# Bulk loads at the change of pass behind small transfers, and one segment's first maxima behind the next group's first products

## The chip, the cores and the metric

One Trainium2 chip, of which one core is used. The metric is the device time of one execution in microseconds, taken in several runs; the time before is the median of three runs. A profile comes from one execution of its own.

TensorE (PE, with its weight loads as PEld), VectorE (DVE), ScalarE (ACT) and GpSimd (POOL) each work through a list of instructions in order. All transfers of this kernel are issued by SyncE (SP), also in order, and run on 16 DMA engines. Semaphores tie the lists together.

## The reference

An attention block with a memory of the earlier segments, and a token-mixing MLP, both behind a layer norm that is scaled and shifted by values computed from a condition `c`:

```python
h = _layernorm(x, axis=-1) * (1 + ca) + sa
x = x + ga * _A_ref(h, A_wq, A_wk, A_wv, A_wo, A_beta)
h = _layernorm(x, axis=-1) * (1 + cb) + sb
x = x + gb * _B_ref(h, B_w1, B_b1, B_w2, B_b2)
```

There are 2048 tokens of 1024 channels. In `_A_ref`, 32 heads of width 32 work on 4 segments of 512 tokens. For each head and segment: causal softmax attention inside the segment; a read of the memory, `phi(q) @ M / phi(q) @ z`; a mix of both by a gate for each head; then the memory takes up this segment's keys and values. `_B_ref` multiplies across tokens, 2048 to 3584 and back, with a gelu between. Everything is float32.

## The kernel before, in words

Float32 precision is got from TensorE's faster formats by splitting: an operand becomes a high and a low part (`split`, lines 115 to 122: ScalarE or VectorE rounds the high part, VectorE or GpSimd subtracts for the low part), and a product is three products: high by high, high by low, low by high.

**Iterations.** The attention stage runs over `its` (line 376): two passes, in each 8 groups of 4 heads, in each group two segments. The first pass (t = 0 to 15) takes the first and second segment, the second pass (t = 16 to 31) the third and fourth. So t = 3 is group 1, segment 1, and t = 4 is group 2, segment 0. Between t = 15 and t = 16 is the change of pass: the normalized input of the third segment must be in the on-chip pages instead of the first's, and the weights of group 0 are loaded again.

**One iteration** consists of:
- `project(t, 0)` and `project(t, 1)`: keys and values of two token tiles each, tile `nps`, made of 8 chunks (`kv_chunk`, line 188) of six products. Chunk k uses page `h` of channel block k and weight tile k // 2. Line 195 is the product.
- `project(t, 2)`: transposes of the keys (`kps`, line 419), the queries (`qps`, line 203), their splits into the tile `sg`, which has one buffer, and for each head the *stack*: `stack(t, h)` (lines 382 to 390) issues three transfers `sk<-sg` of 128 KB (L388, L389, L390) that put the parts of q and k of one head on one set of partitions. `project(t, 3)` has the stack of the last head and prepares the values. There are two sets of `sk` tiles, used by even and odd t in turn.
- `maxima(t, h)` (line 482): for each head the scores are computed once (`sx`, `sy`, `sz`, line 492), only to find each query's maximum with VectorE (line 494). For every two heads the maxima are transposed (`nmps`), split (`nt`), and sent by four small transfers `sk<-nt` of 2 KB (line 507) into two spare rows of `sk`.
- `scores(t, h)` (line 521): the scores again, transposed, with the maxima subtracted through the spare rows (`a`, lines 529, 532, 536), the exponential on ScalarE, a mask by GpSimd, a copy `ph` (line 543, ScalarE) and the low part `p` (line 545, GpSimd).
- `values(t, h)` (line 547): products `pv` of `ph` and `p` with the values (line 563), normalized by VectorE.

**Bulk transfers at the change of pass.** `reload_h(seg, ct)` (line 371) loads one page of 512 KB, queue entry `h<-hT` (L373); eight are a segment. A page of the third segment takes the buffer of a page of the first, so it cannot be loaded before t = 14's products have read that. `load_w` (line 178) loads a group's six weight tiles, `wv<-wsp` and `wq<-wsp` (L170), 512 KB each; weight tiles have eight buffers. `mod_fetch(j)` (line 586) loads 512 KB of the modulation weights, `rawm` (L588), into one of three buffers given out in turn; `mod_late` (line 591) reduces it with VectorE.

**What sets the order.** One Python loop over n (lines 707 to 735) traces the program: for each n `scores(n)`, `maxima(n + 3)`, `values(n - 2)`, perhaps `load_w`, `project(n + 8)`, perhaps `reload_h`, and planned work such as `mod_fetch(2)` at n = 51 and `mod_fetch(3)` at n = 52. The order in which an engine or the queue gets its instructions is not this one: a planner in the compiler lays it, by when it expects inputs and buffers to be ready, earlier traced work first. `with tc.issue_after(x)` keeps what is traced inside the block behind instruction x on x's own engine or queue; it adds no instruction. `last_sk[t, h]` is the last transfer of a stack, `last_nt[t, h]` the last of the four small transfers.

Of the kernel before, what the change touches and what calls it, by code (L numbers as in the profile page):

```python
# [18 lines left out]
P = 128  # L19
NSEG, L = 4, 512  # L20
NK = D // P
# [20 lines left out]
def attention_and_mlp(ctx, tc, x, wq, wkv, wo, beta, w1, b1, w2, b2, c, wm_a, wm_b, out):  # L42
    nc = tc.nc
    V, A, G, T, SY = nc.vector, nc.scalar, nc.gpsimd, nc.tensor, nc.sync
# [143 lines left out]
    def kv_chunk(w, h, half, k, ps):  # L188
        wt = w["v", k // 2]
        o = 256 * (k % 2)  # L190
        n = 6 * k
        for i, j in ((0, 0), (0, 1), (1, 0)):
            for aa in range(2):
                tt = 2 * half + aa
                T.matmul(ps[:, aa], h[:, j, 128 * tt:128 * tt + 128], wt[:, i, o:o + 256],  # L195
                         start=(n == 0), stop=(n >= 6 * NK - 2), skip_group_check=True)
                n += 1

    def q_chunk(w, h, k, ps):
        wt = w["q", k // 4]  # L200
        o = 128 * (k % 4)
        for n, (i, j) in enumerate(((0, 0), (0, 1), (1, 0))):
            T.matmul(ps, wt[:, i, o:o + 128], h[:, j], start=(k + n == 0), stop=(3 * k + n == 3 * NK - 1))  # L203
# [130 lines left out]
    for i in range(2):  # L334
        ps = bank("s2", 2, f"scps{i}")
# [35 lines left out]
    def reload_h(seg, ct):  # L371
        pg = new_page(f"h{seg}_{ct}")
        SY.dma_start(pg.bitcast(F32), hT1[seg - 2, ct])  # L373
        hpages[seg, ct] = pg
# [2 lines left out]
    NI = len(its)  # L377
    st = {}

    last_sk, last_nt = {}, {}  # L380

    def stack(t, h):

# [8 lines left out]
    def project(t, piece):  # L392
        pr, g, seg = its[t]
        if piece == 0:
            st[t] = {}
        w = W[pr, g]
        hp = [hpages[seg, ct] for ct in range(NK)]
        d = st[t]
        if piece in (0, 1):
            if piece == 0:  # L400
                d["k32"] = pj.tile([P, 4, 128], F32, tag="k32", bufs=1, name=f"k32_{t}")
                d["v32"] = pj.tile([P, 4, 132], F32, tag="v32", bufs=1, name=f"v32_{t}")
                G.memset(d["v32"][:, :, 128:132], 1.0)
            half = piece
            k32, v32 = d["k32"], d["v32"]
            if t:
                ps = two_tiles(bank("pj", 2, f"nps{t}_{half}"))
                for k in range(NK):
                    kv_chunk(w, hp[k], half, k, ps)
            else:  # L410
                ps = two_tiles(first[half])
            A.copy(k32[:, 2 * half:2 * half + 2], ps[:, :, 0:128])
            A.copy(v32[:, 2 * half:2 * half + 2, 0:128], ps[:, :, 128:256])
        elif piece == 2:
            k32 = d["k32"]
            d["sg"] = sg = pj.tile([P, 4, L], F32R, tag="sg", bufs=1, name=f"sg{t}")
            ps = bank("pj", 2, f"kps{t}")
            for i in range(4):
                T.transpose(ps[:, 128 * i:128 * i + 128], k32[:, i], ident)
            split(sg[:, 2:4], ps, A, V)  # L420
            if t:
                ps = bank("pj", 2, f"qps{t}")
                for k in range(NK):
                    q_chunk(w, hp[k], k, ps)
            else:
                ps = first[2]
            split(sg[:, 0:2], ps, A, V)
            if seg:
                r = pj.tile([P, L], F32, tag="tmp", bufs=2, name=f"rq{t}")
                A.activation(r, ps, AF.Relu, scale=-1.0)  # L430
                A.activation(r, r, AF.Exp, scale=-1.0)
                d["pq"] = pj.tile([P, L], F32, tag="pq", bufs=1, name=f"pq{t}")
                V.scalar_tensor_tensor(d["pq"], ps, 0.0, r, op0=ALU.max, op1=ALU.add)
            if seg < 3:
                r = pj.tile([P, L], F32, tag="tmp", bufs=2, name=f"rk{t}")
                kf = k32.rearrange("p a n -> p (a n)")
                A.activation(r, kf, AF.Relu, scale=-1.0)
                A.activation(r, r, AF.Exp, scale=-1.0)
                d["pk"] = pj.tile([P, 4, 128], F32, tag="pk", bufs=1, name=f"pk{t}")
                V.scalar_tensor_tensor(d["pk"].rearrange("p a n -> p (a n)"), kf, 0.0, r, op0=ALU.max, op1=ALU.add)  # L440
            for h in range(3):
                stack(t, h)
        else:
            stack(t, 3)
            v = d["v32"][:, :, 0:128].rearrange("p a (h e) -> p a h e", h=4)
            vp = d["vp"] = b.tile([P, 4, 4, NV], BF16, tag="vp", bufs=3, name=f"vp{t}")
            r1 = pj.tile([P, 4, 4, 32], F32, tag="tmp", bufs=2, name=f"r1_{t}")
            G.memset(vp[:, :, :, 0:1], 1.0)
            A.copy(vp[:, :, :, 1:33], v)
            V.tensor_tensor(r1, v, vp[:, :, :, 1:33], op=ALU.subtract)  # L450
            A.copy(vp[:, :, :, 33:65], r1)
            V.tensor_tensor(vp[:, :, :, 65:97], r1, vp[:, :, :, 33:65], op=ALU.subtract)
            memory(t)
# [28 lines left out]
    def maxima(t, h):  # L482
        d = st[t]
        if h % 2 == 0:
            d["mx"] = b.tile([P, 2, 4], F32, tag="mx", bufs=2, name=f"mx{t}_{h}")
        mx = d["mx"]
        q, k = d["sk", h][0:96, 0], d["sk", h][0:96, 1]
        for tiles in ((0, 1), (2,), (3,)):
            s = bank("s1", 2, f"s{'xxyz'[tiles[-1]]}_{t}_{h}")
            outs = [(i, s[:, 128 * i * (len(tiles) - 1):][:, 0:128 * i + 128]) for i in tiles]  # L490
            for i, o in outs:
                T.matmul(o, q[:, 128 * i:128 * i + 128], k[:, 0:128 * i + 128], start=True, stop=True)  # L492
            for i, o in outs:
                marks[4 * t + h - LEADS, "V"] = V.tensor_tensor_reduce(  # L494
                    o, o, mask[:, 384 - 128 * i:], 1.0, -3.0e38, op0=ALU.add, op1=ALU.max,
                    accum_out=mx[:, h % 2, i:i + 1])
        if h % 2 == 0:
            return
        ps = bank("ms", 1, f"nmps{t}_{h}")
        T.transpose(ps[0:8, 0:128], mx.rearrange("p a b -> p (a b)"), ident)  # L500
        nt = [b.tile([8, P], F32R, tag=f"nt{i}", bufs=2, name=f"nt{i}_{t}_{h}") for i in range(2)]
        A.activation(nt[0], ps[0:8, 0:128], AF.Copy, scale=-1.0)
        V.scalar_tensor_tensor(nt[1], ps[0:8, 0:128], -1.0, nt[0].bitcast(F32), op0=ALU.mult, op1=ALU.subtract)
        for hh in range(2):
            sk = d["sk", h - 1 + hh]
            for part in range(2):
                last_nt[t, h] = SY.dma_start(sk[96 + part:97 + part, 0].bitcast(F32).rearrange("p (b n) -> p b n", n=128),
                             nt[part][4 * hh:4 * hh + 4].bitcast(F32))
# [76 lines left out]

    def mod_fetch(j):
        r = a.tile([P, D], F32, tag="raw", bufs=3, name=f"rawm{j}")
        SY.dma_start(r, wm_b[P * j:P * j + P])  # L588
        return r

    def mod_late(j, r):
# [98 lines left out]
    for g in range(2, NG):  # L690
        n = 8 * g - 13
# [7 lines left out]
    for j in range(32):  # L699
        n = 49 + j if j < 8 else ML0 + 2 * j + 8  # L700
        later(n, lambda j=j: mod_fetch(j), n + 1, lambda r, j=j: mod_late(j, r), "V")
    plan(WO0 - 3, lambda: spread(gaw, 0))
    for i in range(8):
        n = WO0 + WOS * i
        later(n, lambda i=i: wo_fetch(i), n + 1, lambda r, i=i: wo_split(i, r), "G")

    for n in range(-LEADS, 4 * NI + VL):
        at(scores, n)
        at(maxima, n + LEADS)
        with behind(n, "P" if n - VL >= 64 else ""):  # L710
            at(values, n - VL)
        m = n + LEADP
        if 0 <= m + 4 < 4 * NI:
            t = (m + 4) // 4
            if its[t][:2] not in W:
                with tc.issue_after(last_sk[t - 2 if t > 16 else 0, 3].ins):
                    load_w(its[t][1], its[t][0])
        if m >= 8:
            at(project, m)
        if 59 <= m < 67:  # L720
            seg, ct = 2 + (m - 59) // 4, 2 * ((m - 59) % 4)
            with ExitStack() as s:
                if seg == 3:
                    s.enter_context(tc.issue_after((last_sk[15, 3] if ct < 4 else last_nt[14, 3]).ins))
                reload_h(seg, ct)
                reload_h(seg, ct + 1)
        if 4 * NI - 5 <= m < 4 * NI + 3:
            i = m - 4 * NI + 5
            for c in (2 * (i % 4), 2 * (i % 4) + 1):
                wop[c, i // 4] = new_page(f"wo{c}_{i // 4}")  # L730
                if c < 5 or i < 4:
                    SY.dma_start(wop[c, i // 4].bitcast(F32), wos[c, i // 4])
        for f, engines in todo.pop(n, ()):
            with behind(n, engines):
                f()
# [14 lines left out]
    w = cw_pool.__enter__()  # L750
# [412 lines left out]
```

## Time and profile before

| | |
|---|---|
| time before, median of 3 runs | 2220.87 us (2216.29 to 2220.99) |
| profiled execution | 2220.33 us, span 2218.6 us |
| mean granted clock of TensorE | 0.998 |
| busy: TensorE, VectorE, ScalarE, GpSimd | 98%, 75%, 51%, 32% of the span |
| DMA | 423.05 MB, mean 191 GB/s |
| attention stage | from about 60 us to about 947 us, pass 2 from about 495 us |

A row of the timeline gives start, duration (for several instructions merged in one row, of all), engine, line, operation, tile written and tiles read, count, and in brackets how long the engine had stood idle before it and what ended that. "SPq" rows are transfers at the time at which the queue issues them; the issue takes the time shown, the landing is later. "Granted clock" is 1.00 at full speed. A stretch's busy time of TensorE can hide slow work: at half clock it is busy and does half.

### The profile page before, as it was taken

What the parts mean: (1) busy time and instruction counts of PE and PEld (TensorE: products, weight loads), DVE (VectorE), ACT (ScalarE), POOL (GpSimd) and SP (SyncE); (2) the same over time, 40 slices, a digit from 0 to 9 for tenths busy, and PEclk for the clock granted to TensorE, in tenths of its full rate; (3) what the DMA queues carried; (4) which work ended last, traced back from release to release, by engine and by line L of the source; (5) the groups of instructions that cost most, each with busy time, mean ns of one, the idle gap of its engine ahead of it and who ended that gap; (6) DMA issues with size and microseconds to landing.
All of it is one profiled execution on the core that took longest, in us unless ns stands there. A gap on an engine that the chain in (4) does not pass through costs nothing.

```text
span 2218.6 us, 38129 instructions
## 1 busy us (share of the span) xinstructions
PE 2183.0 (98%) x13786; PEld 1879.1 (85%) x13786; DVE 1674.1 (75%) x3762; ACT 1132.9 (51%) x2050; POOL 720.0 (32%) x831
## 2 busy tenths in 40 slices
PE   8999999999999999999999999999999999999999
PEld 5988998889999999988888888888888888888887
DVE  7687777767777686755858766888888887969687
ACT  5486876855666666654636533533334242424232
POOL 2175766656667677653002200033330000000000
PEclk9999999999999999999999999999999999999999
DMA  7656665587566666664755686665556541414134
GB/s 287 193 178 195 182 181 167 166 295 249 165 202 194 201 199 183 198 222 133 243 194 195 225 319 250 246 232 206 214 202 223 195 156 58 143 58 147 57 124 152
DMA packets 175184, 423.05 MB, mean 191 GB/s; under 512 B 17524, under 2 KB 71828, under 8 KB 166036
## 3 DMA queue, kind: packets, MB, share of 16 engines
q1 hardware_dynamic: 174996, 420.61, 57.4%
q8 instruction: 110, 1.80, 0.3%
q14 instruction: 78, 0.64, 0.1%
HBM read 244.62 MB, written 125.06 MB: 167 GB/s over the span
## 4 chain that ended last, share of the span: by engine, by line
PE 83%; DVE 7%; DMA 4%; ACT 2%; issue 1%; POOL 1%; SPq 1%; DVEq 0%; ACTq 0%
PE mx L943 48%; PE nps L195 10%; PE po L813 7%; PE qps L203 6%; PE pv L563 3%; DMA rawm<-in_wm_b_dram 2%; PE a L529 1%; PE sz L492 1%; PE sx L492 1%; POOL p L545 1%; DMA sk<-sg 1%; PE a L536 1%; DVE wv L122 1%; PE srow L308 1%; PE a L532 1%
## 5 line engine op out<-in xcount | busy, mean ns | idle before, releaser
L943 PE MATMUL mx<-bU,sp 128*128 128x512 f32 x2352 | 534.4, 389 | 0.9 <-DVE ac L950 0.9
L943 PEld LDWEIGHTS mx<-bU,sp 128*128 128x128 f32 x2352 | 441.1, 188 | 93.7 <-issue 1.3
L119 ACT CAST sp<-wr 128x384 fp32r<-128x384 f32 (+2 forms) x408 | 217.0, 545 | 429.9 <-PE mx L943 354.8
L195 PE MATMUL nps<-wv,h 128*128 128x256 f32 x3072 | 430.5, 283 | 1.5 <-DVE h L122 0.8
L943 PE MATMUL mx<-bA,sp 128*128 128x512 f32 x1764 | 430.5, 389 | 0.0
L545 POOL TENSOR_TENSOR p<-p,ph 128x640 f16<-128x640 f32 x256 | 376.7, 1472 | 119.8 <-ACT ph L543 115.0
L195 PEld LDWEIGHTS nps<-wv,h 128*128 128x128 f32 x3072 | 401.9, 190 | 9.8 <-DVE h L122 2.0
L943 PEld LDWEIGHTS mx<-bA,sp 128*128 128x128 f32 x1764 | 331.1, 188 | 68.7
L122 DVE TENSOR_TENSOR sp<-wr,sp 128x384 fp32r<-128x384 f32 (+2 forms) x408 | 260.4, 649 | 28.3 <-ACT sp L119 28.0
L950 DVE TENSOR_TENSOR ac<-mx,ac 128x512 f32<-128x512 f32 x280 | 190.4, 688 | 84.4 <-PE mx L943 84.0
L203 PE MATMUL qps<-h,wq 128*128 128x512 f32 x768 | 195.8, 398 | 0.0
L543 ACT CAST ph<-p 128x1280 f16<-128x1280 f32 x128 | 161.0, 1258 | 49.5 <-POOL p L541 49.1
L813 PE MATMUL po<-wo,ots 128*128 128x512 f32 x768 | 179.7, 391 | 0.0
L541 POOL TENSOR_SCALAR_AFFINE_SELECT p<-p 128x256 f32<-128x256 f32 x256 | 133.2, 526 | 114.2 <-ACT p L538 65.1
L813 PEld LDWEIGHTS po<-wo,ots 128*128 128x128 f32 x768 | 143.3, 188 | 29.9 <-DVE ots L122 0.4
L943 PE MATMUL mx<-bB,sp 128*128 128x512 f32 x588 | 164.0, 389 | 0.0
L203 PEld LDWEIGHTS qps<-h,wq 128*128 128x128 f32 x768 | 140.2, 188 | 27.1
L943 PEld LDWEIGHTS mx<-bB,sp 128*128 128x128 f32 x588 | 110.4, 188 | 22.9
L950 DVE TENSOR_TENSOR cc<-mx,cc 128x512 f32<-128x512 f32 x140 | 95.0, 685 | 39.4 <-PE mx L943 39.3
L494 DVE CUSTOM_DVE_ANT_0 sz<-sz,mask 128x512 f32<-128x512 f32 x128 | 89.2, 697 | 44.1 <-PE sz L492 43.2
L494 DVE CUSTOM_DVE_ANT_0 sx<-sx,mask 128x128 f32<-128x128 f32 (+1 forms) x256 | 93.6, 366 | 34.5 <-PE sx L492 31.5
L530 ACT ACTIVATE p<-a,shift 128x512 f32<-128x512 f32 x128 | 88.0, 687 | 40.5 <-PE a L529 38.1
(207 smaller groups left out, 3194.1 us busy)
## 6 DMA issues: line engine op xcount, KB each, us to landing
sk<-sg SPq DMA_DIRECT2D x384, 128.0 KB
wr<-in_w_dram SPq DMA_DIRECT2D x28, 1024.0 KB
wr<-in_w_dram SPq DMA_DIRECT2D x32, 768.0 KB
bstu<-ucd SPq DMA_DIRECT2D x28, 768.0 KB
wsp<-wv SPq DMA_DIRECT2D x32, 512.0 KB
rawm<-in_wm_b_dram SPq DMA_DIRECT2D x32, 512.0 KB
wv<-wsp SPq DMA_DIRECT2D x32, 512.0 KB
pcd<-cc SPq DMA_DIRECT2D x14, 1024.0 KB
```

Of the source, the lines that this page charges most:

```text
L119: last_hi[0] = A.copy(hi, src)
L122: return lo_eng.tensor_tensor(lo, src, hi.bitcast(F32), op=ALU.subtract)
L195: T.matmul(ps[:, aa], h[:, j, 128 * tt:128 * tt + 128], wt[:, i, o:o + 256], start=(n == 0), stop=(n >= 6 * NK - 2), skip_group_check=True)
L203: T.matmul(ps, wt[:, i, o:o + 128], h[:, j], start=(k + n == 0), stop=(3 * k + n == 3 * NK - 1))
L494: marks[4 * t + h - LEADS, "V"] = V.tensor_tensor_reduce(o, o, mask[:, 384 - 128 * i:], 1.0, -3.0e38, op0=ALU.add, op1=ALU.max, accum_out= ...
L530: A.activation(p32[:, 0:512], b0, AF.Exp, scale=SCALE, bias=shift)
L541: G.affine_select(w, w, pattern=[[0, 2], [1, 128]], compare_op=ALU.is_ge, fill=0.0, base=0, channel_multiplier=-1)
L543: marks[n, "A"] = A.copy(hi, p32)
L545: marks[n, "G"] = G.tensor_tensor(lo[:, c], p32[:, c], hi[:, c], op=ALU.subtract)
L813: T.matmul(ps, os_[:, i, P * ct:P * ct + P], wop[ct, nh][:, j], start=(n == 0), stop=(n == 3 * NK - 1))
L943: T.matmul(ps, ops[q][:, i, P * k:P * k + P], b[:, j], start=(m == 0 and first), stop=(m == 3 * nk - 1), skip_group_check=True)
L950: V.tensor_tensor(d, ps, d, op=ALU.add)
```

## The change

Four edits, all of order:

1. The eight pages of the third segment are now traced together at m = 59. Pages 0 to 3 are kept behind `last_nt[12, 3]` (the small transfers of t = 12's second pair of heads), pages 4 to 7 behind `last_sk[14, 1]` (the second stack of t = 14). Before, they were traced two at a time at m = 59 to 62 without an edge. The fourth segment's pages keep their edges.
2. The weight tiles of t = 16 are kept behind `last_sk[14, 3]` (the last stack of t = 14) instead of `last_sk[0, 3]`. For the later groups nothing changes.
3. `mod_fetch(2)` and `mod_fetch(3)` are kept behind `last_sk[14, 3]`.
4. `kv_chunk` returns its last product. The products of `maxima(3, 0)` on TensorE (t = 3, the fourth iteration of the stage; its first head) are kept behind the last product of chunk 0 of `project(4, 0)`.

```diff
             if t:
                 ps = two_tiles(bank("pj", 2, f"nps{t}_{half}"))
                 for k in range(NK):
-                    kv_chunk(w, hp[k], half, k, ps)
+                    chunk[t, half, k] = kv_chunk(w, hp[k], half, k, ps)
...
-            for i, o in outs:
-                T.matmul(o, q[:, 128 * i:128 * i + 128], k[:, 0:128 * i + 128], start=True, stop=True)
+            with ExitStack() as st_:
+                if (t, h) == (3, 0):
+                    st_.enter_context(tc.issue_after(chunk[4, 0, 0].ins))
+                for i, o in outs:
+                    T.matmul(o, q[:, 128 * i:128 * i + 128], k[:, 0:128 * i + 128], start=True, stop=True)
...
-        SY.dma_start(r, wm_b[P * j:P * j + P])
+        with ExitStack() as s:
+            if j in (2, 3):
+                s.enter_context(tc.issue_after(last_sk[14, 3].ins))
+            SY.dma_start(r, wm_b[P * j:P * j + P])
...
-                with tc.issue_after(last_sk[t - 2 if t > 16 else 0, 3].ins):
+                with tc.issue_after(last_sk[t - 2, 3].ins):
                     load_w(its[t][1], its[t][0])
...
-        if 59 <= m < 67:
-            seg, ct = 2 + (m - 59) // 4, 2 * ((m - 59) % 4)
-            with ExitStack() as s:
-                if seg == 3:
-                    s.enter_context(tc.issue_after((last_sk[15, 3] if ct < 4 else last_nt[14, 3]).ins))
-                reload_h(seg, ct)
-                reload_h(seg, ct + 1)
+        if m == 59:
+            for ct in range(NK):
+                with tc.issue_after((last_nt[12, 3] if ct < 4 else last_sk[14, 1]).ins):
+                    reload_h(2, ct)
+        if 63 <= m < 67:
+            ct = 2 * (m - 63)
+            with tc.issue_after((last_sk[15, 3] if ct < 4 else last_nt[14, 3]).ins):
+                reload_h(3, ct)
+                reload_h(3, ct + 1)
```

More of the change, by code (lines that the diff above doesn't have):

```diff
@@ L194, in kv_chunk @@
                 tt = 2 * half + aa
-                T.matmul(ps[:, aa], h[:, j, 128 * tt:128 * tt + 128], wt[:, i, o:o + 256],
-                         start=(n == 0), stop=(n >= 6 * NK - 2), skip_group_check=True)
+                mm = T.matmul(ps[:, aa], h[:, j, 128 * tt:128 * tt + 128], wt[:, i, o:o + 256],
+                              start=(n == 0), stop=(n >= 6 * NK - 2), skip_group_check=True)
                 n += 1
+        return mm
     def q_chunk(w, h, k, ps):
@@ L378, in attention_and_mlp @@
     st = {}
-    last_sk, last_nt = {}, {}
+    last_sk, last_nt, chunk = {}, {}, {}
     def stack(t, h):
```

## The prediction

> **What bounds the kernel now.** I read the page's table of engines first, then busy time in stretches of 25 us, then, for the stretches that stand out, the DMA queue's order, the chain that ended last, and the single waits of TensorE.
>
> ```profile
> PE 2183.0 (98%) x13786; PEld 1879.1 (85%) x13786; DVE 1674.1 (75%) x3762; ACT 1132.9 (51%) x2050; POOL 720.0 (32%) x831
> ```
>
> TensorE is busy in 2183.0 of 2218.6 us, so a change of order can win only part of the 35.6 us in which it stands, and what it loses at a lowered clock. Where these lie is read by stretch (columns: stretch, its length, busy us and instructions of PE, PEld, DVE, ACT, POOL, granted clock, DMA share, GB/s).
>
> ```profile
> 125.00:150.00 25.00, 23.42 (x203) 21.45 (x201) 23.41 (x59) 19.66 (x34) 18.33 (x20) 0.93 0.90 275
> 450.00:475.00 25.00, 23.81 (x219) 21.59 (x219) 18.57 (x47) 14.80 (x29) 16.05 (x21) 1.00 1.01 360
> 475.00:500.00 25.00, 20.91 (x158) 18.07 (x157) 12.21 (x38) 12.76 (x22) 11.96 (x14) 0.93 0.70 229
> 444.00:500.00 56.00, 50.73 (x430) 45.36 (x429) 35.91 (x98) 31.30 (x56) 32.56 (x39) 0.97 0.87 295
> ```
>
> From 444 to 500 us TensorE stands for 56.00 - 50.73 = 5.27 us, VectorE and ScalarE are busy for 64% and 56%, and the DMA engines are full (1.01 from 450 to 475). That is the change of pass: the bound there is the DMA queue. Only this stretch and 125 to 150 show a lowered clock (0.93). The queue's own order (start, us that issuing took, what, how many):
>
> ```profile
> 447.99 0.60 SPq L588 DMA_DIRECT2D rawm<-in_wm_b_dram  x1
> 448.64 2.10 SPq L170 DMA_DIRECT2D wv<-wsp  x2
> 451.81 2.10 SPq L588 DMA_DIRECT2D rawm<-in_wm_b_dram  x2
> 454.02 0.79 SPq L373 DMA_DIRECT2D h<-hT  x1
> 454.90 4.95 SPq L507 DMA_DIRECT2D sk<-nt  x4
> 460.37 6.11 SPq L373 DMA_DIRECT2D h<-hT  x7
> 466.57 0.70 SPq L388 DMA_DIRECT2D sk<-sg  x1
> 476.29 2.62 SPq L507 DMA_DIRECT2D sk<-nt  x4
> 483.76 0.59 SPq L390 DMA_DIRECT2D sk<-sg  x1
> 487.18 0.86 SPq L170 DMA_DIRECT2D wv<-wsp  x2
> ```
>
> Five bulk loads of 512 KB and the first page go out ahead of the four small maxima transfers of t=12, and seven more pages go out behind them, ahead of the stacks of t=14. The four small ones need 4.95 us to issue at 454.90, against 2.62 us at 476.29: the queue is held back by what is in flight. The chain that ended last names what this costs (start, us, what):
>
> ```profile
> 128.30 3.87 DMA sk<-sg
> 456.43 7.64 DMA sk<-nt
> 469.67 8.14 DMA sk<-sg
> 486.51 1.55 DMA sk<-nt
> ```
>
> A small transfer that lands in 1.55 us at 486.51 needs 7.64 us at 456.43, and a stack 8.14 us. TensorE's waits behind them, and ScalarE's (last column: idle time before, and who ended it):
>
> ```profile
> 464.21 0.47 PE L529 MATMUL a<-sk 98*128 98x512 f32 x1 [1.19 <-DMA sk<-nt]
> 471.58 0.34 PE L536 MATMUL a<-sk 98*128 98x256 f32 x2
> 473.74 2.42 PE L195 MATMUL nps<-wv,h 128*128 128x256 f32 x19
> 477.94 0.47 PE L492 MATMUL sx<-sk 96*128 96x128 f32 x2 [1.27 <-DMA sk<-sg]
> 489.85 0.61 PE L563 MATMUL pv<-vp,ph 128*128 128x97 bf16 x10 [0.56 <-ACT ph L543]
> 491.33 0.20 PE L563 MATMUL pv<-vp,p 128*128 128x65 bf16 x1 [0.87 <-POOL p L545]
> 493.67 0.36 PE L563 MATMUL pv<-vp,p 128*128 128x65 bf16 x6 [1.38 <-POOL p L545]
> 494.82 0.83 PE L195 MATMUL nps<-wv,h 128*128 128x256 f32 x3
> 488.05 0.59 ACT L119 CAST sg<-kps 128x512 fp32r<-128x512 f32 x1 [4.32 <-DMA sk<-nt]
> ```
>
> The waits of 1.19 and 1.27 us are direct. The next three are one wait further: `sg` has one buffer, so the split of t=15's keys may not write it before the last stack of t=14 (issued at 483.76) has read it. ScalarE stands 4.32 us in front of that split, with the `ph` copy next in its order, then GpSimd's `p`, then TensorE's values. The five waits add up to 1.19 + 1.27 + 0.56 + 0.87 + 1.38 = 5.27 us, the whole idle time of the stretch. The clock, in stretches of 3.4 us:
>
> ```profile
> 129.60:133.00 3.40, 2.16 (x15) 1.50 (x16) 2.79 (x9) 3.40 (x7) 2.06 (x3) 1.00 1.06 256
> 133.00:136.40 3.40, 3.40 (x24) 3.40 (x21) 3.37 (x4) 3.31 (x6) 2.73 (x3) 0.50 1.07 294
> 488.00:491.40 3.40, 1.97 (x19) 1.37 (x17) 2.73 (x6) 3.18 (x5) 1.44 (x2) 1.00 0.84 311
> 491.40:494.80 3.40, 2.02 (x17) 1.57 (x18) 1.67 (x4) 0.44 (x1) 2.93 (x3) 1.00 0.94 313
> 494.80:498.20 3.40, 3.40 (x18) 3.33 (x17) 2.39 (x10) 2.79 (x6) 2.50 (x4) 0.50 1.01 387
> ```
>
> Right behind two thin stretches (2.16 and 2.02 us busy) stands one at half clock: 3.4 us that do the work of 1.7 us.
>
> **The change part by part.** No instruction is added or taken away; the edges order instructions within one queue.
>
> *Pages of the third segment.* Eight loads (4 MB), all put behind t=12's maxima transfers, four of them also behind the second stack of t=14. One load leaves from ahead of the small transfers, four from ahead of the stacks. *Weights and modulation.* The two weight loads at 448.64 and the two `rawm` at 451.81 go behind the last stack of t=14, so four more leave from ahead of the small ones; of the weight group the other four tiles already go out late (487.18 on). Ahead of the small transfers remain one `rawm` and the stores of the last weights. By this the small transfers should land in about the 1.55 us of an open queue plus their 2.62 us of issue, some 459 to 460, against the 464.21 at which the score that waits for them starts: the 1.19 us go. The stacks of t=14 come right behind four pages at some 462 to 464, when `sg` is split (an estimate: seven issues of 0.6 us behind 458), and land before 470, ahead of the 477.94 - 1.27 = 476.7 at which the maxima want them: the 1.27 us go. The later stacks of t=14 then need not wait for the queue but for the scores of t=12, whose last products start at 471.58; then the last stack is issued near 475, some 9 us before 483.76. ScalarE's 4.32 us, and with them 0.56 + 0.87 + 1.38 us, go. I take all 5.27 us. Bounds: nothing (the planner keeps the stacks late) to 5.27.
>
> *The half clock at 494.80.* If the thin stretch before it fills, 1.7 us come back. Bounds: 0 to 1.7; I take 1.7, since the idle time that thins it is the three waits just removed. The Trainium skill, page "TensorE: Matmul & The Clock Gate", Part 1, says that the clock falls to half only after an idle window of about 3.4 us; by that rule gaps of 0.56 to 1.38 us would not have lowered it, their removal would not raise it, and the sum would be 1.7 us smaller. The trace agrees with the length of the window and not with the condition: no gap before 494.80 is over 1.38 us.
>
> *What the bulk meets later.* Behind the last stack of t=14 now stand `rawm` twice and six weight tiles, with a third `rawm` that the buffers let through. The first kv product of t=16 (now at 494.82) needs tile 0, and its fifth chunk, 24 products on, tile 2; at 2.42 / 19 = 0.127 us a product that is 3.1 us later. At 360 GB/s a 512 KB load takes 1.46 us; tile 2 is at worst the sixth, so it lands 6 x 1.46 + 1.55 = 10.3 us behind the last stack. Issued near 475, that is 485.3; the product then starts near 494.82 - 6.97 = 487.9 and wants tile 2 at 491.0: over 5 us of cover, price 0. Without the earlier stacks (483.76) it lands at 494.1, against 494.82 - 2.46 + 3.1 = 495.5: hidden still. Behind the edges wait also the maxima transfers of t=13's second pair, on the same queue, by one `rawm` (1.46 us) at most; they follow the last stack today, and would follow it earlier.
>
> *VectorE's part of `rawm`.* Two of its passes move from a stretch with idle time into the next one, which is nearly full:
>
> ```profile
> L592 DVE SCALAR_TENSOR_TENSOR rawm<-rawm,scb 128x1024 f32<-128x1024 f32 x5 | 7.7, 1532 | 0.0
> 500.00:521.00 21.00, 19.95 (x187) 18.84 (x185) 19.55 (x52) 13.07 (x23) 15.31 (x19) 1.00 0.81 247
> ```
>
> VectorE is busy in 19.55 of 21 us there, and TensorE stands for 1.05. Two passes of 1.53 us are 3.06 us more, against ScalarE's 4.32 us that VectorE no longer waits for. Bounds 0 to 3.06; I take 1.0 us, a third of the way, since the earlier start gives more room than the passes fill.
>
> *The fourth segment's first maxima.* Four products (`sx` twice, `sy`, later `sz`) go behind the first six kv products of t=4.
>
> ```profile
> 132.30 0.47 PE L492 MATMUL sx<-sk 96*128 96x128 f32 x2 [1.01 <-DMA sk<-sg]
> 133.41 3.48 PE L195 MATMUL nps<-wv,h 128*128 128x256 f32 x16
> 132.08 3.30 DVE L122 TENSOR_TENSOR wv<-rawv,wv 128x512 fp32r<-128x512 f32 x2 [0.61 <-ACT wv L119]
> 153.48 1.14 PE L474 MATMUL up<-v,pk 128*128 128x132 f32 x8 [0.95 <-DVE pv L566]
> ```
>
> The hole of 1.01 us before `sx` is not free for them: the fifth and sixth need the low half of the weights, which VectorE finishes about halfway through its 3.30 us, at some 133.7. So the maxima start near 134.0 instead of 132.30, and behind them in TensorE's order wait the next products. Best case: hole and half clock both go, -2.7 us. Worst case: TensorE stands to 133.7, 1.4 us more, and the clock still falls. I take 0, because VectorE sets this stretch: it is busy in 23.41 of the 25 us to 150, and TensorE's next stop, at 153.48, waits 0.95 us for VectorE. What TensorE wins at 133 it waits for at 152; if that cover goes, the two ends above are its price.
>
> The profiled execution took 2220.33 us (span 2218.6 and 1.7 around it), near the median of 2220.87. Sum: 2220.33 - 5.27 - 1.70 + 1.0 + 0 = 2214.4 us.
>
> **The rivals.** (a) *The stacks stay late.* The order is laid by the planner, and an edge only says "behind". If only the two DMA waits go, the gain is 1.19 + 1.27 = 2.46 us: 2217.9. For it: the third stack also waits for the scores of t=12. Against it: from 460.37 to 476.29 the queue itself held everything up. (b) *The clock stays low*: the waits go, and the half-clock stretch comes elsewhere. For it: 488.00 to 491.40 is as thin (1.97 us) and the next stretch ran at full clock, so thinness alone does not decide. 2214.4 + 1.7 = 2216.1. The rule of the Trainium skill named above would come to the same time. (c) *A worse order, slower.* The edge at t=4 sits in front of everything up to the change of pass, and the planner may lay all of it anew. What an order is worth shows here:
>
> ```profile
> 150.00:450.00 300.00, 293.36 (x2627) 267.24 (x2626) 219.80 (x636) 222.31 (x416) 191.58 (x221) 1.00 0.62 177
> ```
>
> Now TensorE stands for 6.64 us in these twelve stretches, 0.55 each; 125 to 150 shows 1.58. If a new order made all twelve like that one, it would cost 12 x 1.58 - 6.64 = 12.3 us: 2214.4 + 12.3 = 2226.7. It decides from 10.9 us on (1.46 a stretch). Against it: the edge moves four products by less than 2 us, into a stretch that VectorE sets. (d) *The other end of the first maxima*: nothing is hidden and both half clocks go: 2214.4 - 2.7 = 2211.7.
>
> **How the numbers follow.** Change as forecast 0.45 (2214.4, alone 2212 to 2217), (a) 0.21, (b) 0.08, (c) 0.19, (d) 0.07. 0.2% (4.4 us, about what a measurement of this kernel can tell from no change) sets the bounds 2216.4 and 2225.3. Most of the forecast, all of (d) and half of (b) and a little of (a) are faster: 0.52. The rest of (a) and (b), and a quarter of (c), make "same" 0.32; (c) beyond its point 0.16. The range runs from 2209.5, somewhat under (d), to 2225, where (c) begins to be slower.
>
> **What would show it.** In the queue: the four small transfers of t=12 issued within about 3 us near 455, pages behind them, the last stack of t=14 before 477. In TensorE's waits: no wait for `sk` between 444 and 500, none over 0.5 us for `ph` or `p`; ScalarE's 4.32 us gone; clock 1.00 through 498. At 130: `sx` behind six kv products, waiting for `wv` instead of `sk`, and the same stop near 152. Wrong would be: a last stack still issued after 481, a wait for `wv`, `wq` or `h` at the first products of t=16, VectorE's waits for `rawm` ahead of maxima, or more idle time than 6.64 us between 150 and 450.

## The result, and the profile after

The changed kernel takes 2225.85 us (median of 15 runs, 2221.14 to 2230.38); the kernel before took 2220.99 in the runs beside it (15 runs, 2216.29 to 2226.14). The ratio is 1.0018, with a 95% interval of 1.001 to 1.0026. So it is slower, by about the 0.2% within which the prediction called a kernel "same", and clearly not faster. Predicted were 2214.4 us, range 2209.5 to 2225.0; the median lies 0.85 us above that range.

The profiled execution after took 2225.85 us, span 2223.0, which is 4.4 us longer than the span before. Where they lie is read by stretch. First three rows of before that the prediction did not show (columns: stretch, length, busy us and instructions of PE, PEld, DVE, ACT, POOL, granted clock, DMA share, GB/s):

```profile
500.00:525.00 25.00, 23.95 (x211) 22.05 (x209) 20.31 (x54) 13.92 (x24) 18.14 (x21) 1.00 0.81 252
525.00:550.00 25.00, 25.00 (x250) 23.66 (x249) 18.78 (x65) 17.70 (x32) 13.64 (x18) 1.00 0.83 263
900.00:925.00 25.00, 23.84 (x223) 22.03 (x222) 17.39 (x53) 18.00 (x32) 17.43 (x21) 1.00 0.66 210
```

The same view of the kernel after:

```profile
125.00:150.00 25.00, 22.26 (x200) 19.34 (x199) 22.55 (x59) 19.07 (x33) 19.25 (x21) 1.00 0.89 275
150.00:450.00 300.00, 293.44 (x2624) 267.23 (x2624) 219.80 (x634) 222.32 (x415) 190.53 (x221) 1.00 0.61 176
444.00:500.00 56.00, 54.54 (x487) 49.65 (x487) 40.26 (x110) 35.69 (x63) 39.02 (x44) 1.00 0.87 289
500.00:525.00 25.00, 21.19 (x171) 19.30 (x171) 15.47 (x50) 10.55 (x18) 14.46 (x17) 0.86 0.79 255
525.00:550.00 25.00, 23.91 (x236) 22.32 (x235) 18.50 (x55) 17.31 (x32) 14.59 (x18) 1.00 0.87 275
900.00:925.00 25.00, 22.44 (x198) 20.14 (x198) 12.87 (x45) 15.76 (x27) 13.55 (x17) 0.93 0.66 179
```

Take as the loss of a stretch the time in which TensorE stands, plus (1 - clock) times the length. At the change of pass (444 to 500) it falls from 5.27 + 1.68 to 1.46: 5.5 us won. In the 25 us behind, it rises from 1.05 to 3.81 + 3.50: 6.3 us lost. From 525 to 550 another 1.1 us are lost, and from 900 to 925 3.1 us (1.16 to 2.56 + 1.75). From 125 to 150 it falls by 0.6 us (1.58 + 1.75 to 2.74). These five make -5.5 + 6.3 + 1.1 + 3.1 - 0.6 = 4.4 us. That this equals the longer span is in part chance: between 550 and 900 TensorE stands another 1.9 us longer (5.09 against 3.18), and the measure charges 0.8 us twice, in which TensorE stood while its clock was lowered. So the gain that was forecast came at the change of pass, and was more than given back behind it, most of it in two places.

The queue of after shows the first half (start, us of issuing, what, count):

```profile
455.54 2.62 SPq L511 DMA_DIRECT2D sk<-nt  x4
458.25 1.81 SPq L374 DMA_DIRECT2D h<-hT  x4
...
473.94 0.59 SPq L391 DMA_DIRECT2D sk<-sg  x1
474.58 2.98 SPq L374 DMA_DIRECT2D h<-hT  x4
477.61 0.43 SPq L595 DMA_DIRECT2D rawm<-in_wm_b_dram  x1
...
503.84 0.60 SPq L391 DMA_DIRECT2D sk<-sg  x1
504.48 1.08 SPq L374 DMA_DIRECT2D h<-hT  x2
505.66 0.38 SPq L595 DMA_DIRECT2D rawm<-in_wm_b_dram  x1
```

The small transfers go out in 2.62 us, pages behind them; the last stack of t=14 is issued at 473.94 instead of 483.76. The last three rows are the other half: a modulation tile, `rawm` 6, is issued only at 505.66, behind all stacks of t=15 and two pages. In the kernel before it is issued at 489.55. The two tiles that the change holds back, 2 and 3, hold back those that follow: three buffers are given out in turn, so tile 6 takes tile 3's, which is free only when the pass over tile 3 ends at 495.8; the queue's order adds the rest. VectorE takes its instructions in order, and the pass over tile 6 stands, as before the change, between the two halves of a product that others wait for:

```profile
508.18 0.20 DVE L468 RECIPROCAL rdd<-rdd 128x8 f32<-128x8 f32 x1
512.17 1.23 DVE L599 SCALAR_TENSOR_TENSOR rawm<-rawm,scb 128x1024 f32<-128x1024 f32 x1 [3.79 <-DMA rawm<-in_wm_b_dram]
513.32 0.42 DVE L469 TENSOR_TENSOR am<-rd,rdd 128x256 f32<-128x256 f32 x1
```

The last row is what everyone waits for: the second half of t=15's product `am` (line 469, in `memory`). Its reciprocal is ready at 508.4, but it stands behind the pass. It is the reader that frees the one PSUM buffer `ms`, which TensorE's next product `up` (line 475) writes. TensorE's rows, and its clock in stretches of 3.4 us:

```profile
509.66 0.42 PE L496 MATMUL sy<-sk 96*128 96x384 f32 x1
513.89 2.10 PE L475 MATMUL up<-v,pk 128*128 128x132 f32 x8 [3.81 <-DVE am L469]
```

```profile
509.70:513.10 3.40, 0.38 (x6) 0.12 (x1) 0.93 (x1) 1.26 (x1) 0.97 (x3) 1.00 1.00 398
513.10:516.50 3.40, 2.61 (x11) 2.55 (x12) 2.59 (x13) 0.48 (x2) 0.45 (x2) 0.50 1.01 404
516.50:519.90 3.40, 3.40 (x13) 2.83 (x13) 2.87 (x10) 1.55 (x4) 3.40 (x4) 0.50 0.11 43
```

One late transfer of 512 KB costs a wait of 3.79 us on VectorE, 3.81 us on TensorE, and then 6.8 us at half clock, another 3.0 to 3.4. The chain that ended last holds three such tiles one after another (start, us, what):

```profile
477.61 7.01 DMA rawm<-in_wm_b_dram
486.63 9.94 DMA rawm<-in_wm_b_dram
505.66 6.49 DMA rawm<-in_wm_b_dram
```

The second place lies 400 us later, in code that no edit touches:

```profile
914.75 0.45 PE L540 MATMUL a<-sk 98*128 98x256 f32 x2 [2.56 <-ACT p L534]
```

### The profile page after: what moved, and what is told of

It is laid out like the page before. It is cut to its first block, busy times and chain, and to the rows that moved or that the text cites. A ratio compares the mean times of both kernels' runs of the same rounds, so it can differ in the third digit from the quotient of the medians.

```text
span 2223.0 us, 38090 instructions
## 1 busy us (share of the span) xinstructions
PE 2183.4 (98%) x13786; PEld 1878.8 (85%) x13786; DVE 1668.3 (75%) x3762; ACT 1130.9 (51%) x2050; POOL 722.0 (32%) x831
## 4 chain that ended last, share of the span: by engine, by line
PE 80%; DVE 7%; DMA 4%; ACT 4%; issue 2%; POOL 2%; SPq 1%; DVEq 0%; ACTq 0%; POOLq 0%
PE mx L952 48%; PE nps L195 10%; PE qps L204 7%; PE po L822 4%; PE pv L567 3%; DMA rawm<-in_wm_b_dram 2%; PE a L533 1%; PE sz L496 1%; DMA h<-x1d 1%; POOL p L549 1%; PE sx L496 1%; DVE wv L122 1%; PE a L540 1%; PE a L536 1%; PE srow L309 1%
## 5 line engine op out<-in xcount | busy, mean ns | idle before, releaser
L195 PE MATMUL nps<-wv,h 128*128 128x256 f32 x3072 | 424.2, 282 | 4.3 <-DVE wv L122 1.6
L195 PEld LDWEIGHTS nps<-wv,h 128*128 128x128 f32 x3072 | 396.1, 189 | 12.2 <-DVE wv L122 2.2
```

The costliest lines, as they stand in the source:

```text
L195: mm = T.matmul(ps[:, aa], h[:, j, 128 * tt:128 * tt + 128], wt[:, i, o:o + 256], start=(n == 0), stop=(n >= 6 * NK - 2), skip_group_check ...
```

## The experiments

All times are medians; each ratio is to the kernel before on the same chip, with its 95% interval. The theories, by the letters that the expectations use: *M*, the chain of modulation tiles just described (edit 3) is the loss. *X*, the edit of the first maxima (edit 4) is the loss, through the order that the planner writes. *W*, pages and weights come too late for t=16. *D*, the late transfers are the loss by sharing the queues, wherever the passes over them stand.

### Edit 3 taken out, edit 3 alone, edit 4 alone, edit 4 taken out

First, the changed kernel without edit 3:

```
     def mod_fetch(j):
-        with ExitStack() as s:
-            if j in (2, 3):
-                s.enter_context(tc.issue_after(last_sk[14, 3].ins))
-            SY.dma_start(r, wm_b[P * j:P * j + P])
+        SY.dma_start(r, wm_b[P * j:P * j + P])
```

> The changed kernel with the edit of the modulation tiles undone (tiles 2 and 3 are fetched as early as before); pages, weights and first maxima stay changed. Theory M (the delayed tiles 2 and 3 push tiles 4 to 7 back through the three buffers, tile 6 lands at 512.1, and VectorE's 3.8 us wait for it holds the product of tile 15 and then the clock): VectorE waits under 0.5 us for any modulation tile in 500 to 525, no half clock at 513, TensorE's matmul time and idle time there are back at the sum of before, and the time is 2214 to 2218 us, that is 0.1% to 0.3% under before. Rival X (the first maxima's edit, through the order that the planner writes, is the loss): still about 2225. Rival W (pages and weights come too late for tile 16): still 2222 to 2226, with TensorE's waits in 500 to 525 released by transfers of pages or weights.

Measured: 2216.97 us, ratio 0.9985 (0.9973 to 0.9997). Its stretches, and all that TensorE (444 to 500) and VectorE (444 to 530, for modulation tiles) waited for there (us, times, longest):

```profile
444.00:500.00 56.00, 53.77 (x488) 49.66 (x488) 41.48 (x112) 37.12 (x66) 38.86 (x44) 1.00 0.88 295
500.00:525.00 25.00, 25.00 (x235) 22.91 (x234) 20.07 (x63) 13.85 (x27) 12.30 (x18) 1.00 0.93 313
```

```profile
PE a L533 <- DMA sk<-nt: 2.2, 1, 2.2
PE nps L195 <- DVE wv L122: 0.3, 1, 0.3
DVE rawm L596 <- DMA rawm<-in_wm_b_dram: 0.7, 1, 0.7
```

As M says: TensorE is busy for all of 500 to 525 at full clock. VectorE is busy for 20.07 us there and holds nothing up. X and W fall.

Then edit 3 by itself (the kernel before, with that block added):

> The kernel before with the edit of the modulation tiles alone. Theory M: modulation tile 6 is behind the stacks of tile 15 and two pages of the last segment again, VectorE waits 2 to 4 us for it between 505 and 515, the product of tile 15 waits behind it, and the time is 2222 to 2227 us (the gain at the change of pass is not there to set against it, but the page-and-weight queue may already be late enough to shift it by 1 to 2 us). Rivals X and W: the time of before, 2219 to 2222, with no wait over 1 us for a modulation tile in 500 to 525.

Measured: 2230.15 us, ratio 1.0043 (1.0025 to 1.006), slower than either theory said. The wait is there, but at tile 2, earlier than expected. VectorE's row and then TensorE's:

```profile
485.63 1.23 DVE L597 SCALAR_TENSOR_TENSOR rawm<-rawm,scb 128x1024 f32<-128x1024 f32 x1 [6.70 <-DMA rawm<-in_wm_b_dram]
487.59 0.69 PE L494 MATMUL sy<-sk 96*128 96x384 f32 x1 [4.72 <-DVE mx L496]
```

This time maxima stand behind the pass in VectorE's order, and with 6.70 us the wait is worse: the seven pages that edit 1 would have moved still stand ahead of the stacks of t=14, and tile 2, behind the last of these, is issued at 481.57 instead of 477.61. The mechanism is M's, the place is not: which tile hurts depends on what else is in the queue. It explains only part of the loss: against before, this run loses 5.2 us more between 444 and 525, and a stop of 4.00 us near 660 with a clock of 0.80 over the 25 us from 650 costs about nine more in its profile (the slowest of its 8 runs).

Edit 4 alone (the kernel before, with the `issue_after` on `chunk[4, 0, 0]` around the products of t=3's first head):

> The kernel before with the edit of the first maxima alone. Theory M: about no change, 2219.5 to 2222, the half clock at 133 gone and a hole of about 1 us in the kv products at 133 in its place, and TensorE's stop ahead of the last up-product at 153 still there. Rival X: 2223 to 2226.

Measured: 2221.49 us, ratio 1.0002 (0.9991 to 1.0013). The row for 125 to 150:

```profile
125.00:150.00 25.00, 22.25 (x199) 19.70 (x199) 23.62 (x59) 19.76 (x35) 18.95 (x21) 1.00 0.87 271
```

The half clock is gone (1.75 us) and TensorE stands for 1.17 us more. X falls.

The changed kernel without edit 4:

> The changed kernel with the edit of the first maxima undone. Theory M: VectorE's wait of 3 to 4 us for modulation tile 6 and the half clock at 513 stand as in the changed kernel, 2224 to 2227 us. Rival X: both are gone and the time is 2214 to 2218.

Measured: 2224.26 us, ratio 1.0017 (1.0005 to 1.0029), the changed kernel's loss in full. The stop is there again:

```profile
512.33 2.10 PE L475 MATMUL up<-v,pk 128*128 128x132 f32 x8 [3.73 <-DVE am L469]
```

### Where the pass over a late tile stands

Is it the late transfer, or the place of its pass in VectorE's order? First, all four edits, with the passes over tiles 6 and 7 planned later:

```
-        later(n, lambda j=j: mod_fetch(j), n + 1,
+        later(n, lambda j=j: mod_fetch(j), n + (3 if j in (6, 7) else 1),
               lambda r, j=j: mod_late(j, r), "V")
```

> The changed kernel, all four edits, with the passes of modulation tiles 6 and 7 put three iterations behind their fetch in place of one; VectorE's order up to the product of tile 15 is otherwise that of the changed kernel, and tile 6 is fetched as late. Theory M (it is the place of a late tile's pass in VectorE's order that costs, not the late transfer): tile 6 still lands at about 511 to 513, but VectorE no longer waits for it ahead of the product of tile 15, TensorE has no stop over 1.5 us in 500 to 520, no half clock there, and 475 to 525 is 5 to 6.5 us shorter than in the changed kernel. The time is then 2216 to 2221, at the lower end if the stop and half clock at 912 are gone too, at the upper end if they stay. Rival D (the late transfers themselves, sharing the queues with stacks of tile 15, are the loss): 2223 to 2227, with TensorE waiting for stacks in 500 to 520.

Measured: 2222.34 us, ratio 1.0016 (1.0005 to 1.0027). The stop before `up` is gone, and another is there (VectorE's row, then TensorE's):

```profile
496.01 1.32 DVE L599 SCALAR_TENSOR_TENSOR rawm<-rawm,scb 128x1024 f32<-128x1024 f32 x1 [2.36 <-DMA rawm<-in_wm_b_dram]
500.60 0.79 PE L496 MATMUL sz<-sk 96*128 96x512 f32 x1 [2.54 <-DVE mx L498]
```

Now tile 3's pass holds up maxima. VectorE's instructions stand in the same order up to there as in the changed kernel, where that wait was 1.08 us; here it is 2.36, and the clock from 500 to 525 is 0.86 again. The test is clean for tile 6 (its pass moved, its stop went), and a miss for the time. In part the next late tile takes its place, since tiles 2 and 3 are still late; the two stops differ by who waits for VectorE, not in kind. In part the loss lies behind: between 525 and 900 TensorE stands for 9.15 us, against 3.18 before, with stops of 2.55 us at 684.6 and 2.02 us at 855.1, each with a lowered clock behind it. M doesn't cover that part.

Second, only tile 3 held back (`if j == 3:` in place of `if j in (2, 3):`). In the order written for this, tile 6's pass stands behind both halves of `am`:

> The changed kernel with only modulation tile 3 held back, tile 2 fetched as early as before. Tile 6 uses tile 3's buffer, so it is still late; in the order written here its pass stands behind both halves of the product of tile 15. Theory M: tile 6 still lands at 508 or later, no stop over 1.5 us of TensorE in 500 to 520, no half clock there, 2214 to 2220 us. Rival D: 2223 to 2227 with the stop there.

Measured: 2221.26 us, ratio 1.0015 (1.0006 to 1.0024), above what M said. VectorE's rows, and the stretches:

```profile
507.73 0.41 DVE L469 TENSOR_TENSOR am<-rd,rdd 128x256 f32<-128x256 f32 x1
512.67 1.44 DVE L599 SCALAR_TENSOR_TENSOR rawm<-rawm,scb 128x1024 f32<-128x1024 f32 x1 [1.06 <-DMA rawm<-in_wm_b_dram]
```

```profile
444.00:500.00 56.00, 53.35 (x472) 48.70 (x471) 38.24 (x105) 35.48 (x63) 37.51 (x43) 0.97 0.84 282
500.00:525.00 25.00, 25.00 (x220) 23.16 (x219) 20.91 (x61) 13.73 (x26) 13.49 (x18) 1.00 0.94 308
```

Tile 6 is as late as in the changed kernel (512.67 against 512.17), and from 500 to 525 nothing is lost: a late tile whose pass stands behind `am` costs nothing there. That rules D out for this stretch. What is lost lies before it: one stop of 2.65 us for `sk<-nt` and a half-clock window. Against before the two stretches are 3.7 us better, and yet the profiled execution takes the same 2220.24 us: the 3.7 us are lost further on, in many stops of which none is over 1.4 us. M doesn't cover this either. So both runs show what the stop at 513 comes from, but in neither does the time fall to that without edit 3 (0.9985): of the kernels here, none that holds back tile 2 or 3 by an edge is under 1.0015.

### What the other edits are worth

Edits 1 and 2, without 3 and 4:

> The kernel before with the edits of pages and weights alone (no modulation edit, no edit of the first maxima). If the first maxima's edit is worth nothing by itself, this is within 1.5 us of the run without the modulation edit (2216.97), so 2215.5 to 2218.5; if that edit helps through the half clock it takes away at 133, this is about 1.7 us slower than that run, 2218 to 2219; if it costs, it is 2213 to 2215.5.

Measured: 2217.54 us, ratio 0.9994 (0.9985 to 1.0002).

```profile
444.00:500.00 56.00, 54.97 (x497) 50.64 (x496) 42.21 (x114) 37.99 (x66) 39.80 (x45) 1.00 0.90 301
```

TensorE stands for 1.03 us in the change of pass. What edit 3 adds there is read with edit 4 alike on both sides. Without edit 4, the run with edit 3 has this row:

```profile
444.00:500.00 56.00, 55.38 (x497) 50.64 (x496) 40.99 (x112) 36.55 (x66) 38.27 (x44) 1.00 0.85 288
```

That is 0.62 us against 1.03; with edit 4 it is 1.46 against 2.23. So edit 3 brought 0.4 to 0.8 us there, little of the 5.27.

Edit 1 alone:

> The kernel before with the edit of the pages alone. If the pages are the bulk that stood in the way of the transfers at 460 to 480, most of the gain is here: the stops at 462 to 492 and the half clock at 495 are gone but for one or two of them, and the time is 2215 to 2219. If the weights (six transfers that started at the end of the previous pass) were the larger part, the stops for the values' stack of tile 14 stay and the time is 2219 to 2222.

Measured: 2219.60 us, ratio 0.9999 (0.999 to 1.0007): nothing. Its profile shows TensorE standing for 2.84 us from 444 to 500 (a single stop for `sk<-nt`, near 460) at a clock of 0.97, so the weights count too.

### Passes and fetches planned later, without an edge

If a late tile only costs where its pass keeps its old place, both should be moved in the plan, without any edge:

```
-        n = 49 + j if j < 8 else ML0 + 2 * j + 8
+        n = 49 + j + (3 if j >= 2 else 0) if j < 8 else ML0 + 2 * j + 8
```

with edits 1, 2 and 4.

> The edits of pages, weights and first maxima, with no wait on the modulation tiles; in its place the fetches and the passes of tiles 2 to 7 are together planned three iterations later, so the tiles are out of the change of pass as the change wanted, and VectorE's order is written with it. Theory M (late tiles cost only where their passes keep the old place in VectorE's order): no VectorE wait over 1 us for a modulation tile in 444 to 530, no stop of TensorE over 1.5 us in 444 to 525, clock 1.00 in both stretches, and 2213 to 2217 us. If moving six passes of 1.2 to 2.4 us into 500 to 545 costs by VectorE's busy time after all (the +1.0 with an end of 3.06 of the prediction), 2217 to 2220.

Measured: 2217.13 us, ratio 0.9987 (0.9978 to 0.9996), faster than both kernels. No wait of VectorE for a modulation tile is left between 444 and 560, and:

```profile
444.00:500.00 56.00, 53.30 (x481) 48.78 (x480) 37.00 (x105) 37.06 (x64) 37.52 (x45) 1.00 0.85 277
500.00:525.00 25.00, 25.00 (x231) 22.56 (x231) 18.74 (x60) 13.51 (x26) 12.27 (x17) 1.00 0.91 307
```

That is M's number and M's profile. But the fetches did not all move with the passes. The queue's rows:

```profile
451.45 2.69 SPq L592 DMA_DIRECT2D rawm<-in_wm_b_dram  x2
505.70 4.05 SPq L592 DMA_DIRECT2D rawm<-in_wm_b_dram  x3
```

Tiles 2 and 3 are still issued at 451.45, ahead of the small transfers as before (451.81); only their passes moved, from 471.06 and 481.63 to 495.32 and 503.06. Tiles 5 to 7 moved on both sides: they are issued from 505.70 on (before: 488.56 to 492.40), with passes at 517.51, 523.85 and 530.28 (before: 500.70, 509.50 and 515.17). So the run shows that later passes cost nothing here, and that late tiles cost nothing with a later pass; it does not show what tiles 2 and 3 would do if both their fetch and their pass came later. It is no better than leaving edit 3 out altogether (2216.97): the tiles need not be moved at all. Five iterations later instead of three:

> As the last run, but five iterations later. Theory M: the same, 2213 to 2217 us. By VectorE's busy time: 2217 to 2221, or more where the tiles 6 and 7 meet tile 8.

Measured: 2229.02 us, ratio 1.0044 (1.0027 to 1.0061), a plain miss. Neither stretch explains it: 2.87 us of standing from 444 to 500, none from 500 to 525. What TensorE waited for between 600 and 1000 us does, first before, then here:

```profile
PE a L529 <- DMA sk<-nt: 0.4, 1, 0.4
```

```profile
PE a L533 <- DMA sk<-nt: 10.2, 5, 3.8
```

The largest of the five, in the queue's rows and TensorE's:

```profile
647.48 0.45 SPq L592 DMA_DIRECT2D rawm<-in_wm_b_dram  x1
648.02 0.66 SPq L667 DMA_DIRECT2D wor<-in_wo_dram  x1
648.73 0.47 SPq L592 DMA_DIRECT2D rawm<-in_wm_b_dram  x1
...
650.00 2.64 SPq L511 DMA_DIRECT2D sk<-nt  x4
```

```profile
657.26 0.76 PE L533 MATMUL a<-sk 98*128 98x512 f32 x1 [3.81 <-DMA sk<-nt]
```

Three bulk loads ahead of four small transfers: the picture of the old change of pass, made anew by the planner some 200 us further on. The kernel before has its four small transfers of that point at 645.74 and the bulk only from 651.85. With edit 3 alone the same stop is there, 4.00 us at 661.32. So the order of the rest changes with these edits too, and can cost more than the place that they are meant for.

Last, three iterations later without edit 4:

> Three iterations later, with the edits of pages and weights alone. Beside the run with the first maxima's edit it tells what that edit is worth here: within 1.5 us if nothing; the prediction put it at 0 with ends of 2.7 us faster and 1.4 us slower.

Measured: 2219.01 us, ratio 0.9991 (0.9981 to 1.0001), 1.9 us above the run with edit 4, with intervals that overlap: edit 4 is worth nothing that these runs can tell.

### All runs side by side

Loss in 444 to 525 us (standing plus lowered clock, as above) of the profiled execution, against the ratio of the runs:

| kernel | standing | clock | sum, us | ratio |
|---|---|---|---|---|
| before | 6.32 | 1.68 | 8.0 | 1 |
| all four edits | 5.27 | 3.50 | 8.8 | 1.0018 |
| 1, 2, 4 | 2.23 | 0 | 2.2 | 0.9985 |
| 3 | 8.04 | 5.11 | 13.2 | 1.0043 |
| 4 | 6.14 | 1.68 | 7.8 | 1.0002 |
| 1, 2, 3 | 4.35 | 3.50 | 7.9 | 1.0017 |
| all, passes 6 and 7 later | 2.82 | 3.50 | 6.3 | 1.0016 |
| all, only tile 3 held back | 2.65 | 1.68 | 4.3 | 1.0015 |
| 1, 2 | 1.03 | 0 | 1.0 | 0.9994 |
| 1 | 4.54 | 1.68 | 6.2 | 0.9999 |
| 1, 2, 4, shift by 3 | 2.70 | 0 | 2.7 | 0.9987 |
| 1, 2, 4, shift by 5 | 2.87 | 1.68 | 4.6 | 1.0044 |
| 1, 2, shift by 3 | 2.16 | 0 | 2.2 | 0.9991 |

The four kernels that lose least here are the four fastest. But the sizes don't carry over: edits 1 and 2 win 7.0 us in this stretch and 1.3 us in the ratio (between 3.3 won and 0.4 lost). The profile of that kernel is the fastest of its 11 runs (2213.67), that of before lies in the middle of its own, so part of the difference is which execution was profiled. The profiles of edit 3 alone and of the shift by 5 are the slowest of their 8 and 6 runs, and that with passes 6 and 7 later is 5.4 us above its median, so their losses are on the high side.

## Why the prediction was wrong

*Pages and weights, 5.27 us, and the half clock, 1.70 us.* Right in the profile. The small transfers go out in 2.62 us, the last stack of t=14 at 473.94, TensorE waits for no `sk` in the stretch, and the clock is 1.00. With these two edits alone the stretch 444 to 525 is 7.0 us better, against 5.27 + 1.70 = 6.97 in the sum. The runs keep less of it: a ratio of 0.9994 is 1.3 us (with edit 4 beside it, 0.9985 is 3.3 of 5.8 us); where the rest goes is not settled. Rivals (a) and (b) fell.

*Modulation, counted in one sum with the weights.* Here the working went wrong first: the 5.27 us were put down to three edits together, and the third had little share in them (with edit 4, 2.23 us are left without it and 1.46 with it; without edit 4, 1.03 and 0.62).

*VectorE's part of `rawm`, +1.0 us with ends of 0 and 3.06.* This is the step that failed. It let two passes move into the nearly full stretch behind 500 us, and priced them by their busy time, 1.53 us each. No pass moved there: three start between 500 and 525 before (500.70, 509.50, 515.17) and after (500.68, 512.17, 518.16); those of tiles 2 and 3 moved only to 484.63 and 494.54. Nor was busy time the price: in the run with the passes planned three iterations later, four lie between 500 and 525, and nothing is lost there. The price is an in-order wait: a pass kept its place in VectorE's order while its tile came later, and the tile behind it by the turn of three buffers, tile 6, later still. In place of +1.0 stand 3.81 us of standing and 3.50 us of lowered clock, 6.3 us more than this stretch lost before; with edit 3 left out, TensorE stands for none of it. The prediction named "VectorE's waits for `rawm` ahead of maxima" as a sign of being wrong (it came, and TensorE stood 1.19 us for maxima at 499.06), and bounded the step at 3.06 all the same, because it counted only the two tiles that the edit names, and not the four behind them in the same buffers.

*What the bulk meets later, 0.* Right for weights: TensorE waits for none of the weight tiles that were moved; its one wait for `wv` between 444 and 500, 0.27 us at 444.61, comes before they are issued. The third `rawm` that was mentioned there was followed as a transfer of 1.46 us in the queue, not as the tile that an engine waits for.

*First maxima, 0.* Right: 1.0002 (0.9991 to 1.0013) alone. The half clock is gone, and VectorE takes back what TensorE wins, as the working had it, though sooner: TensorE waits for it 0.79, 0.63 and 0.46 us at 133.45, 141.15 and 145.29, and the product that began at 153.48 before begins at 153.69.

*Rival (c), a worse order.* Its place was wrong: from 150 to 450 TensorE stands for 6.56 us, against 6.64. That the measured time is near its 2226.7 us is chance: that figure counted standing in this stretch, where none was added. Its kind was right: behind the change of pass the order is another one, and the 3.1 us lost from 900 to 925 look to be of that sort. There `p` stands on ScalarE behind a split that waits for a transfer:

```profile
908.43 0.58 SPq L806 DMA_DIRECT2D otr<-oT  x1
```

```profile
912.82 1.14 ACT L119 CAST ots<-otr 128x512 fp32r<-128x512 f32 x2 [2.10 <-DMA otr<-oT]
```

Before, that transfer was issued at 905.43, and TensorE did not stop for `p` between 900 and 925. The stop and a half-clock window behind it stand in both kernels with edits 1, 2 and 3 as the change has them (2.56 and 2.42 us), and edit 3 alone has one of 2.85 us, also with a half-clock window behind it; with edits 1 and 2 but without 3 the stop for `p` there is at most 1.5 us and the clock 1.00. That it comes from the order is read from these rows; no run was made that changes only this.

*The clock.* The rule of the Trainium skill, page "TensorE: Matmul & The Clock Gate", Part 1, that an idle window of about 3.4 us is what lowers the clock, is not what the trace shows: half clock from 915.9 on followed a stop of 2.56 us, in a window in which TensorE was still busy for 1.16 us. The loss behind a stop was left out of the bounds of the VectorE step, and made up half of it.

## What to carry to other kernels

When a fetch is held back, follow its buffers round: later tiles in the same ring come later too, and the engine that consumes them waits at the old place of each pass, with everything that stands behind it. Leave both where they are, or at least give the pass of a late tile a later place too (here that took the stop away, but with the fetch still held back it did not win the time back). Price the move by the first instruction behind the pass that another engine waits for, not by the pass's busy time. And try each edit of a set by itself: here the two that carried the gain at the change of pass were hidden by one that had little share in it. Then look at the rest of the program as well: losses of 3 us and more came up to 400 us behind the edits.

## What was not expected of the hardware

A stop of 3.81 us cost two windows at half clock, not one: in the 3.4-us window in which the stop ended TensorE was busy for 2.61 of 3.40 us at clock 0.50, and the next one, busy throughout, ran at 0.50 as well. The length of a stop does not settle its price. One of 2.23 us in the run without edit 3, and one of 2.46 us at 544.4 in the run with edits 1 and 2 alone, lowered the clock not at all. One of 2.65 us in the run with only tile 3 held back lowered it to 0.93 over 25 us, one window's worth. One of 2.54 us in the run with passes 6 and 7 later lowered it to 0.86, two windows' worth, and one of 4.00 us with edit 3 alone to 0.80, three. A stop of between 2 and 3 us can thus cost 0, 1.7 or 3.4 us more, which is as much as most of the edits here bring. What decides between them stays open.
